# Operands of an expert layer's matmuls laid at an offset that changes from block to block, with two result buffers instead of three

## The chip, the cores and the metric

The kernel runs on one core of a Trainium2 chip, as one launch. The metric is device microseconds of the whole program, the median of three runs. TensorE multiplies, ScalarE (ACT) and VectorE (DVE) do elementwise work, GpSimd (POOL) issues the gathers and scatters by row index, SyncE (SP) issues the other transfers.

## The reference

Three layers in a row over 8 batches of 576 tokens, 512 wide: a linear attention, a mixture of experts of which each token takes two, and a soft mixture. The change lies in the second:

```python
for e in range(E):                       # 8 experts, w1[e] 512 x 1024, w2[e] 1024 x 512
    for k in range(2):
        mask = top2[:, k] == e
        h = np.maximum(x[mask] @ w1[e], 0.0)
        out[mask] += top2_w[mask, k, None] * (h @ w2[e])
```

Everything is float32. The kernel reaches that precision with three cheaper products: each factor is split into a rounded high part and the low rest, and high x high, low x high and high x low are added.

## The kernel before, in words

The routing makes lists of token rows, by expert. A block is the work of one expert on two tiles of 128 rows (three tiles in the blocks called three-tile blocks, which take in odd tiles). There are ten such blocks mixed in with the attention of later batches, then up to eight three-tile blocks under nested conditions, then fourteen blocks and up to sixteen more under conditions. How many run depends on the data.

One block, `block(b, n_s, n, n_n)` at line 872, goes through eight weight slices `u`. Slices 0 to 3 are the first layer: `hidden` (line 822) multiplies a quarter of w1 with the transposed rows `xh`, `xl`, 24 matmuls of 256 columns a slice, with the weights as the stationary operand and the rows as the moving one. ScalarE writes the high part `hh` (line 833) and VectorE the low part `hl` (line 834); with both, the PSUM bank is free again. In a three-tile block `hidden1` (line 836) does the third tile's rows, 12 matmuls a slice. There are three PSUM banks for these products, taken in turn, so that in a three-tile block the third tile's matmuls of slice 1 write the bank that `hh` and `hl` of slice 0 have read. Slices 4 to 7 are the second layer: `result` (line 854) multiplies `hh`, `hl` (stationary) with a quarter of w2 (moving), 12 matmuls of 512 columns a slice for two tiles.

Each weight slice comes by DMA into a ring, and `split` (line 793) makes its two parts in one of three slots R0, R1, R2: ScalarE the high part `R0h`, VectorE the low part `R0l` (line 797). A slice takes the next slot, eight slices a block, so the order of the slots in a block repeats after three blocks. The next block's rows are gathered by index into `xg`, transposed on TensorE at slice 6 (line 815), and written to `xh`, `xl`.

At the end of a block, or inside the next one, `scatter` (line 862) scales a tile's result out of PSUM into a buffer `y` (VectorE, line 865), and GpSimd adds the buffer to the rows of the output in HBM (line 866). Pool `yp` has three buffers `y`; a new one waits until the scatter that reads its buffer has landed. Three-tile blocks do all their scatters at their own end.

The order of instructions on the engines comes from a scheduler that goes by the code's order, the tiles' dependencies and a model of times. Memory is taken in the order in which tiles are named (lines 767 to 777), each size rounded up to 32 bytes per partition: h and R2, then two small tiles of 32 bytes each, x, `xg0` with 2080 and one of 32 bytes, R0, R1, `xg1`.

Of the kernel before, what the change touches and what calls it, by code (L numbers as in the profile page):

```python
# [11 lines left out]
F32 = mybir.dt.float32  # L12
F16 = mybir.dt.float16
FR = mybir.dt.float32r
I32 = mybir.dt.int32
# [6 lines left out]
P = 128  # L22
B, H, S, DH = 8, 8, 576, 64
D = H * DH
# [6 lines left out]
XC = D + E  # L31


NPA, NPB, NST, NTR = 10, 30, 14, 8
# [710 lines left out]
def experts(k, att, rs):  # L745

    nc, tc = k.nc, k.tc
    with ExitStack() as ctx:
        wp = ctx.enter_context(tc.tile_pool(name="wp", bufs=1, side="right", reuse_waits="tile"))
        yp = ctx.enter_context(tc.tile_pool(name="yp", bufs=2, side="right", reuse_waits="tile"))  # L750
# [4 lines left out]
        def bank(n, shape):  # L755
            b = banks[n]
            b.append(b.pop(0))
            return b[-1][0].tile(shape, F32, name=b[-1][1])
# [5 lines left out]
        w1 = k.w1.rearrange("e (c p) (u f) -> e u p c f", p=P, f=256)  # L764
        w2 = k.w2.rearrange("e (u c p) d -> e u p c d", c=2, p=P)
        tile = lambda n, s, d=FR: wp.tile([P] + s, d, name=n)
        hh, hl = [tile(f"h{h}", [8, 256]) for h in "hl"]
        R = [[None, None] for _ in range(NR)]
        R[2] = [tile(f"R2{h}", [1024]) for h in "hl"]
        gn, gc = [tile(n, [3], F32) for n in ("gn", "gc")]  # L770
        xh, xl = [tile(f"x{h}", [4, 256]) for h in "hl"]

        xg = [tile("xg0", [XC], F32)]
        nb = wp.tile([1, 2], I32, name="nb")
        R[0] = [tile(f"R0{h}", [1024]) for h in "hl"]
        R[1] = [tile(f"R1{h}", [1024]) for h in "hl"]
        xg.append(tile("xg1", [XC], F32))
        x3, h3 = [], []
        nc.vector.memset(gn, 0.0)
        regs = [nc.sync.alloc_register(f"er{i}") for i in range(2)]  # L780
# [17 lines left out]

        ys, late, puts = [], [], {}

        THREE = NPA + NPB + 1

        def at(b, s):
            t, c = (k.idxa, 2 * b + s) if b < NPA else (k.idx, 2 * (b - NPA) + s) if b < THREE else (k.idx3, 3 * (b - THREE) + s)
            return t[:, c:c + 1]
# [3 lines left out]

        def xpose(b, s):  # L810
            pt = bank("ph", [P, 4, P])
            h, l = [x[:, :, s * P:(s + 1) * P] for x in (xh, xl)] if s < 2 else x3
            rows = xg[s] if b else k.xg0[s]
            for c in range(4):
                nc.tensor.transpose(pt[:, c, :], rows[:, c * P:(c + 1) * P], k.ident)  # L815
            nc.scalar.activation(h, pt, AF.Copy)
            last = nc.vector.tensor_sub(l, pt, h.bitcast(F32))
            sc = yp.tile([P, E], F32, name="sc")
            with tc.issue_after(last.ins):
                nc.vector.scalar_tensor_tensor(sc, rows[:, D:XC], 1.0, k.eoha[:, b, :] if b < NPA else k.eoh[:, b - NPA, :], op0=ALU.mult, op1=ALU.mult, accum_out=gn[:, s:s + 1])  # L820

        def hidden(b, u):

            w = [x.rearrange("p (c f) -> p c f", c=4) for x in slot[b, u]]
            ph = bank("ph", [P, 2, 256])
            for g in range(2):
                n = 0
                for c in range(4):
                    for (i, x) in ((0, xh), (0, xl), (1, xh)):
                        nc.tensor.matmul(ph[:, g, :], w[i][:, c, g * P:(g + 1) * P], x[:, c, :], start=n == 0, stop=n == 11)  # L830
                        n += 1
            fs = slice(2 * u, 2 * u + 2)
            nc.scalar.activation(hh[:, fs, :], ph, AF.Relu)  # L833
            nc.vector.scalar_tensor_tensor(hl[:, fs, :], ph, 0.0, hh[:, fs, :].bitcast(F32), op0=ALU.max, op1=ALU.subtract)  # L834
# [18 lines left out]

        def result(b, u, py):
            w = [x.rearrange("p (c f) -> p c f", c=2) for x in slot[b, u]]
            order = [(f, s) for f in range(2) for s in range(len(py))]
            for f, s in order if u < 7 else sorted(order, key=lambda x: x[1]):
                a = [x[:, 2 * (u - 4) + f, s * P:(s + 1) * P] for x in (hh, hl)] if s < 2 else [x[:, 2 * (u - 4) + f, :] for x in h3]
                for (n, (h, i)) in enumerate(((0, 0), (0, 1), (1, 0))):
                    nc.tensor.matmul(py[s], a[h], w[i][:, f, :], start=u == 4 and f == n == 0, stop=u == 7 and f == 1 and n == 2)  # L860

        def scatter(b, s, py):
            y = yp.tile([P, D], F32, name="y", bufs=3)
            ys.append(y)
            nc.vector.tensor_scalar(y, py, gc[:, s:s + 1], None, op0=ALU.mult)  # L865
            d = nc.gpsimd.indirect_dma_start(out=k.x2[:NTOK // 2] if b < NPA else k.x2, out_offset=bass.IndirectOffsetOnAxis(ap=at(b, s), axis=0), in_=y, in_offset=None, compute_op=ALU.add)  # L866

            for o in puts.get(b, []):
                tc.declare_no_dep(d.ins, o.ins, reason="other rows")
            puts.setdefault(b, []).append(d)  # L870

        def block(b, n_s, n, n_n):

            expert(n)
            for s in range(n_n):
                gather(n, s)

            ahead = [(b, 2), (b, 3), (b, 4), (b, 5), (b, 6), (b, 7), (n, 0), (n, 1)]
            if n_s == 3:
                ahead = [(b, 2, 2), (b, 3, 0), (b, 4, 1), (b, 7, 2), (b, 5, 0), (b, 6, 1), (n, 0, 0), (n, 1, 1)]  # L880
            for u in range(8):
                split(*ahead[u])
                if u == 0:
                    load(n, 0)
                    load(n, 1)
                if u < 6:
                    load(n, ahead[u][1])
                if u < 4:
                    hidden(b, u)
                    if n_s == 3:  # L890
                        hidden1(b, u)
                else:
                    if u == 4:
                        py = [bank(f"py{s}", [P, D]) for s in range(n_s)]
                    if u == XU:
                        for s in range(n_n):
                            xpose(n, s)
                    result(b, u, py)
                if u == 1:
                    finish()  # L900
                    nc.vector.tensor_copy(gc, gn)
                yield
            late.extend((b, s, py[s]) for s in range(n_s))
            if b == NPA - 1 or b >= NPA + NST - 1:
                finish()

        def finish():
            while late:
                scatter(*late.pop(0))

        def whole(*a):
            for _ in block(*a):
                pass
# [6 lines left out]
        for s in range(2):  # L920
            xpose(0, s)
        n_steps, n_parts, n_done = len(MIX.split()), 0, 0
        for b in range(NPA):
            if b == NPA - 1:
                nc.gpsimd.tensor_copy(nb, ys[-1][0:1, 0:2].bitcast(I32))
                nc.gpsimd.tensor_copy(nb, k.nb)
            for _ in block(b, 2, *((b + 1, 2) if b + 1 < NPA else (THREE, 3))):
                n_parts += 1
# [20 lines left out]
        with ExitStack() as more:  # L949
            for i in range(NTR):  # L950
                more.enter_context(tc.If(n_threes > i))
                whole(THREE + i, 3, THREE + i + 1, 3)
        threes.close()
# [385 lines left out]
@with_exitstack  # L1339
def attention_moe_softmoe(ctx: ExitStack, tc: tile.TileContext, q, k, v, w_gate, w_noise, noise, w1, w2, phi, m1, m2, out):  # L1340
    s = K()
    s.tc, s.nc = tc, tc.nc
    s.q, s.k, s.v, s.w_gate, s.w_noise, s.noise, s.w1, s.w2 = q, k, v, w_gate, w_noise, noise, w1, w2
    s.phi, s.m1, s.m2, s.out = phi, m1, m2, out
    dp = ctx.enter_context(tc.tile_pool(name="dram", bufs=1, space=DRAM))
    s.xtab = dp.tile([NTOK + NFREE * P, XC], F32, name="xtab")
    s.x2 = dp.tile([NTOK + NFREE * P, D], F32, name="x2")
    s.ctx, s.n_regs = ctx, 0
    consts(s, ctx)
    att = attention(s)  # L1350
    next(att)
    rs = ctx.enter_context(tc.tile_pool(name="rs", bufs=1, side="right", reuse_waits="tile"))
    experts(s, att, rs)
    tail(s, rs, s.rg)
# [49 lines left out]
```

## Time and profile before

| | |
|---|---|
| median of three runs | 1219.99 us (1219.71 to 1221.48) |
| the profiled execution | 1222.69 us, its span 1221.0 us |
| TensorE, weight loads | 1125.1 and 984.7 us busy (92%, 81%) |
| VectorE, ScalarE, GpSimd | 799.3, 570.8, 324.6 us busy (65%, 47%, 27%) |
| mean granted clock of TensorE | 0.967 of full speed |
| blocks of two tiles alone | from about 647 to 1090 us |

A row of a group of instructions names engine, line, operation, what is written from what, and the shape. Matmuls are pipelined: one lasts longer than the distance to the next one's start, and it is the distance that counts for the time. The profile's "busy" of TensorE is thus not a measure of its rate. In the chain of waits each piece is work, or a wait for a transfer, that the end of the program depended on.

### The profile page before, as it was taken

The numbers are of one execution on the slowest core, as the hardware profiler recorded it, in microseconds if no ns is written. First come the engines' busy times: TensorE is split into PE (matmuls) and PEld (weight loads), VectorE is DVE, ScalarE is ACT, GpSimd is POOL, SyncE is SP. The second block draws the span as 40 slices with busy tenths as digits, with TensorE's granted clock in tenths as the row PEclk, the third lists the DMA queues.
The fourth block names the chain that finished last, engine by engine and source line by source line (L and its number), as shares of the span: only waits on it lengthen the run. The fifth ranks groups of instructions, "written<-read, shape, count | busy, mean of one in ns | idle before, by whom it ended". The sixth has DMA issues, their size and how long they took to land. (4 is left out here: it accounts for less than half of the span.)

```text
span 1221.0 us, 21167 instructions
## 1 busy us (share of the span) xinstructions
PE 1125.1 (92%) x7804; PEld 984.7 (81%) x7804; DVE 799.3 (65%) x1383; ACT 570.8 (47%) x877; POOL 324.6 (27%) x348
## 2 busy tenths in 40 slices
PE   2898859999999999999989999999999999969994
PEld 1787759998889999888968998998998998956542
DVE  7899778666976665554546666666666666645653
ACT  3575355465544544334434454544454454424324
POOL 4442153222244222211223322322321321210000
PEclk8899779999999999999999999999999999988997
DMA  9998162875536566555667564563745253237797
GB/s 327 297 318 306 45 207 77 242 227 157 141 84 189 135 199 172 139 149 163 174 184 249 138 202 106 150 195 84 223 110 173 47 148 84 43 66 295 265 356 310
DMA packets 116104, 219.08 MB, mean 179 GB/s; under 512 B 13968, under 2 KB 54032, under 8 KB 111888
## 3 DMA queue, kind: packets, MB, share of 16 engines
q1 hardware_dynamic: 98944, 177.11, 42.3%
q0 software_dynamic: 17040, 40.44, 16.8%
q8 instruction: 67, 1.10, 0.4%
q14 instruction: 53, 0.43, 0.1%
HBM read 243.31 MB, written 49.70 MB: 240 GB/s over the span
## 5 line engine op out<-in xcount | busy, mean ns | idle before, releaser
L797 DVE TENSOR_TENSOR R1l<-ringS,R1h 128x1024 fp32r<-128x1024 f32 x96 | 117.8, 1227 | 105.8 <-ACT R1h L797 103.3
L797 DVE TENSOR_TENSOR R0l<-ringS,R0h 128x1024 fp32r<-128x1024 f32 x95 | 116.8, 1229 | 100.8 <-ACT R0h L797 100.5
L797 ACT ACTIVATE R1h<-ringS 128x1024 fp32r<-128x1024 f32 x96 | 101.9, 1061 | 144.3 <-PE py L860 85.1
L797 DVE TENSOR_TENSOR R2l<-ringS,R2h 128x1024 fp32r<-128x1024 f32 x91 | 112.0, 1231 | 84.1 <-ACT R2h L797 81.7
L797 ACT ACTIVATE R0h<-ringS 128x1024 fp32r<-128x1024 f32 x95 | 100.8, 1061 | 137.9 <-PE py L860 77.0
L797 ACT ACTIVATE R2h<-ringS 128x1024 fp32r<-128x1024 f32 x91 | 96.5, 1061 | 136.2 <-PE py L860 75.1
L830 PE MATMUL ph<-xl,R0h 128*128 128x256 f32 x400 | 111.7, 279 | 1.5 <-issue 1.5
L830 PE MATMUL ph<-xh,R0h 128*128 128x256 f32 x400 | 112.0, 280 | 1.0 <-DVEq L949 1.0
L830 PE MATMUL ph<-xh,R0l 128*128 128x256 f32 x400 | 111.5, 279 | 0.0
L834 DVE SCALAR_TENSOR_TENSOR hl<-ph,hh 128x512 fp32r<-128x512 f32 x140 | 95.7, 684 | 23.2 <-ACT hh L833 23.2
L830 PE MATMUL ph<-xh,R1h 128*128 128x256 f32 x360 | 101.1, 281 | 8.1 <-DVE sc L820 7.6
L742 POOL DMA_INDIRECT xg<-xtab,pl_idx x40 | 50.3, 1257 | 215.9 <-DVE sc L820 197.6
L830 PE MATMUL ph<-xh,R2h 128*128 128x256 f32 x360 | 100.9, 280 | 0.5 <-DVE hl L834 0.5
L830 PE MATMUL ph<-xl,R1h 128*128 128x256 f32 x360 | 100.7, 280 | 0.0
L830 PE MATMUL ph<-xh,R1l 128*128 128x256 f32 x360 | 100.5, 279 | 0.0
L830 PE MATMUL ph<-xl,R2h 128*128 128x256 f32 x360 | 100.5, 279 | 0.0
L830 PE MATMUL ph<-xh,R2l 128*128 128x256 f32 x360 | 100.3, 279 | 0.0
L866 POOL DMA_INDIRECT x<-y,pl_idx x40 | 64.1, 1602 | 127.9 <-DVE y L865 117.8
L833 ACT ACTIVATE hh<-ph 128x512 fp32r<-128x512 f32 x140 | 81.6, 583 | 31.7 <-PE ph L830 31.7
L860 PE MATMUL py<-R1l,hh 128*128 128x512 f32 x200 | 79.7, 398 | 0.0
L860 PE MATMUL py<-R1h,hl 128*128 128x512 f32 x200 | 79.0, 396 | 0.0
L830 PEld LDWEIGHTS ph<-xh,R0h 128*128 128x128 f32 x400 | 75.7, 189 | 2.3 <-issue 1.6
(441 smaller groups left out, 3011.0 us busy)
## 6 DMA issues: line engine op xcount, KB each, us to landing
ringS<-in_moe_w_dram SPq DMA_DIRECT2D x292, 512.0 KB
ringA<-in_moe_w_dram SPq DMA_DIRECT2D x12, 1024.0 KB
ringA<-in_moe_w_dram SPq DMA_DIRECT2D x22, 512.0 KB
xtab<-xr SPq DMA_DIRECT2D x36, 256.0 KB
kt<-in_k_dram SPq DMA_DIRECT2D x8, 1024.0 KB
v<-in_v_dram SPq DMA_DIRECT2D x8, 1024.0 KB
x<-z SPq DMA_DIRECT2D x5, 1280.0 KB
ringS<-x SPq DMA_DIRECT2D x5, 1024.0 KB
```

The costliest lines, as they stand in the source:

```text
L742: k.nc.gpsimd.indirect_dma_start(out=x, out_offset=None, in_=k.xtab[:n], in_offset=bass.IndirectOffsetOnAxis(ap=idx, axis=0))
L797: turn[1:] = [nc.scalar.activation(r[0], f, AF.Copy), nc.vector.tensor_sub(r[1], f, r[0].bitcast(F32))]
L830: nc.tensor.matmul(ph[:, g, :], w[i][:, c, g * P:(g + 1) * P], x[:, c, :], start=n == 0, stop=n == 11)
L833: nc.scalar.activation(hh[:, fs, :], ph, AF.Relu)
L834: nc.vector.scalar_tensor_tensor(hl[:, fs, :], ph, 0.0, hh[:, fs, :].bitcast(F32), op0=ALU.max, op1=ALU.subtract)
L860: nc.tensor.matmul(py[s], a[h], w[i][:, f, :], start=u == 4 and f == n == 0, stop=u == 7 and f == 1 and n == 2)
L866: d = nc.gpsimd.indirect_dma_start(out=k.x2[:NTOK // 2] if b < NPA else k.x2, out_offset=bass.IndirectOffsetOnAxis(ap=at(b, s), axis=0), i ...
```

## The change

The tiles `xh`, `xl` grow by 128 elements (512 bytes) and `hh`, `hl` too. Block `b` uses a view of them that starts 16 elements (64 bytes) times 0 to 7 into the tile: for the rows that number is `b % 8` (7 for the three-tile blocks and for the block behind them), for the first layer's outputs `(3 * b + b // 8) % 8` (0 for the three-tile blocks). The small tiles go to the end, so that h, R2, x, R0 and R1 all start at one remainder by 512 bytes. To make room, `y` has two buffers instead of three.

```diff
-        hh, hl = [tile(f"h{h}", [8, 256]) for h in "hl"]
+        ht = [tile(f"h{h}", [2048 + 128]) for h in "hl"]
         R = [[None, None] for _ in range(NR)]
         R[2] = [tile(f"R2{h}", [1024]) for h in "hl"]
-        gn, gc = [tile(n, [3], F32) for n in ("gn", "gc")]
-        xh, xl = [tile(f"x{h}", [4, 256]) for h in "hl"]
-
-        xg = [tile("xg0", [XC], F32)]
-        nb = wp.tile([1, 2], I32, name="nb")
+        xt = [tile(f"x{h}", [1024 + 128]) for h in "hl"]
         R[0] = [tile(f"R0{h}", [1024]) for h in "hl"]
         R[1] = [tile(f"R1{h}", [1024]) for h in "hl"]
-        xg.append(tile("xg1", [XC], F32))
+        xg = [tile(f"xg{s}", [XC], F32) for s in range(2)]
+        gn, gc = [tile(n, [3], F32) for n in ("gn", "gc")]
+        nb = wp.tile([1, 2], I32, name="nb")
+
+        def x_of(b):
+            o = 16 * (7 if b == NPA or b >= THREE else b % 8)
+            return [x[:, o:o + 1024].rearrange("p (c t) -> p c t", c=4) for x in xt]
+
+        def h_of(b):
+            o = 16 * (0 if b >= THREE else (3 * b + b // 8) % 8)
+            return [h[:, o:o + 2048].rearrange("p (f t) -> p f t", f=8) for h in ht]
+
+        THREE = NPA + NPB + 1
...
-            h, l = [x[:, :, s * P:(s + 1) * P] for x in (xh, xl)] if s < 2 else x3
+            h, l = [x[:, :, s * P:(s + 1) * P] for x in x_of(b)] if s < 2 else x3
...
+            (xh, xl), (hh, hl) = x_of(b), h_of(b)
...
+            hh, hl = h_of(b)
...
-            y = yp.tile([P, D], F32, name="y", bufs=3)
+            y = yp.tile([P, D], F32, name="y", bufs=2)
```

No engine's instructions change their order. What does change is what a `y` waits for. On VectorE, at the end of a three-tile block, before (`DMASW` and a number is one of the counters that scatters and gathers raise when they land; 4700 to 4702 are the results of the three tiles):

```order
L797 TENSOR_TENSOR R1l<-ringS,R1h 128x1024 [waits DMAHW0_49,Activation_49]
L865 TENSOR_SCALAR y<-py_4700,gc 128x512 [waits DMASW0_49,PE_49]
L865 TENSOR_SCALAR y<-py_4701,gc 128x512 [waits DMASW1_49,PE_49]
L865 TENSOR_SCALAR y<-py_4702,gc 128x512 [waits DMASW2_49,PE_49]
L949 COMPARE_AND_BRANCH
L901 COPY gc<-gn 128x3 [waits DVE_49]
L797 TENSOR_TENSOR R2l<-ringS,R2h 128x1024 [waits DMAHW1_49,Activation_49]
L834 SCALAR_TENSOR_TENSOR hl<-ph,hh 128x512 [waits Activation_49]
```

and of the change:

```order
L805 TENSOR_TENSOR R1l<-ringS,R1h 128x1024 [waits DMAHW0_49,Activation_49]
L873 TENSOR_SCALAR y<-py_4700,gc 128x512 [waits DMASW1_49,PE_49]
L873 TENSOR_SCALAR y<-py_4701,gc 128x512 [waits DMASW2_49,PE_49]
L873 TENSOR_SCALAR y<-py_4702,gc 128x512 [waits DMASW6_49,DVE_49,PE_49]
L957 COMPARE_AND_BRANCH
L909 COPY gc<-gn 128x3 [waits DVE_49]
L805 TENSOR_TENSOR R2l<-ringS,R2h 128x1024 [waits DMAHW1_49,Activation_49]
L841 SCALAR_TENSOR_TENSOR hl<-ph,hh 128x512 [waits Activation_49]
```

The order is the same. The third `y` waits for a counter of a later transfer: the scatter of the first `y` of the same block, where it was one of the block before.

## Rows read from the trace of the kernel before

**Rows 1.** Windows: stretch, then busy us of each engine, clock, DMA share, GB/s

```profile
647.00:1090.00 443.00, 440.32 (x2892) 398.53 (x2890) 286.76 (x402) 216.44 (x266) 120.14 (x105) 1.00 0.50 135
```

**Rows 2.** Chain of waits, 660 to 760 us: start, us, what

```profile
671.12 10.89 PE ph L830 x96
682.00 3.21 PE py L860 x14
...
685.54 2.33 PE py L860 x10
...
688.42 5.56 PE py L860 x24
693.97 11.21 PE ph L830 x96
...
717.18 11.31 PE ph L830 x96
```

**Rows 3.** TensorE in order of time, 700 to 705 us: start, duration, what

```profile
699.95 0.28 PE L830 MATMUL ph<-xl,R2h 128*128 128x256 f32 x1
...
702.18 0.28 PE L830 MATMUL ph<-xh,R2l 128*128 128x256 f32 x1
702.30 0.28 PE L830 MATMUL ph<-xh,R0h 128*128 128x256 f32 x1
...
704.91 0.28 PE L830 MATMUL ph<-xh,R0l 128*128 128x256 f32 x1
```

**Rows 4.** TensorE in order of time, 758 to 763 us

```profile
758.09 0.39 PE L860 MATMUL py<-R1h,hl 128*128 128x512 f32 x1
...
760.19 0.40 PE L860 MATMUL py<-R1h,hl 128*128 128x512 f32 x1
...
761.58 0.39 PE L860 MATMUL py<-R2h,hl 128*128 128x512 f32 x1
...
762.72 0.39 PE L860 MATMUL py<-R2l,hh 128*128 128x512 f32 x1
```

**Rows 5.** Groups by line and shape: count, then busy us, mean ns, idle before

```profile
L830 PE MATMUL ph<-xh,R0h 128*128 128x256 f32 x400 | 112.0, 280 | 1.0 <-DVEq L949 1.0
...
L830 PE MATMUL ph<-xh,R1h 128*128 128x256 f32 x360 | 101.1, 281 | 8.1 <-DVE sc L820 7.6 <-DVE bf L490 0.3 <-DVE hl L834 0.2
L830 PE MATMUL ph<-xh,R2h 128*128 128x256 f32 x360 | 100.9, 280 | 0.5 <-DVE hl L834 0.5
```

**Rows 6.** VectorE in order of time, 543 to 554 us, a three-tile block's end

```profile
545.42 0.75 DVE L865 TENSOR_SCALAR y<-py,gc 128x512 f32<-128x512 f32 x1 [0.49 <-PE py L860]
...
546.51 1.23 DVE L797 TENSOR_TENSOR R2l<-ringS,R2h 128x1024 fp32r<-128x1024 f32 x1
548.88 0.69 DVE L834 SCALAR_TENSOR_TENSOR hl<-ph,hh 128x512 fp32r<-128x512 f32 x1 [1.15 <-ACT hh L833]
```

**Rows 7.** GpSimd in order of time, 543 to 554 us

```profile
544.55 1.62 POOL L866 DMA_INDIRECT x<-y,pl_id  x1 [26.22 <-DVE y L865]
```

**Rows 8.** TensorE in order of time, 551 to 553 us

```profile
552.21 0.28 PE L843 MATMUL ph<-R1h,x3h 128*128 128x256 f32 x1
```

**Rows 9.** Line 866, the first scatter at 508.9 us, then at 580.2 us

```profile
DMA to landing us min/median/max: 6.0/6.0/6.0
...
DMA to landing us min/median/max: 4.8/4.8/4.8
```

**Rows 10.** Chain of waits, 440 to 640 us; last, VectorE in order of time

```profile
615.93 0.44 POOL x L866
...
619.74 10.69 DMA x<-y,pl_id
...
637.25 0.52 PE ph L815 x3
...
616.78 0.75 DVE L865 TENSOR_SCALAR y<-py,gc 128x512 f32<-128x512 f32 x1 [0.48 <-PE py L860]
```

**Rows 11.** DMA issues: tiles, queue, count, median us to landing

```profile
x<-y,pl_idx POOLq DMA_INDIRECT x40, 4.9
```

More of the change, by code (lines that the diff above doesn't have):

```diff
@@ L799, in experts @@
         ys, late, puts = [], [], {}
-        THREE = NPA + NPB + 1
         def at(b, s):
```

## The prediction, made before the change was run

> **What bounds the kernel now.** I read first the busy times by stretch, then the chain of waits, then single engines in order of time. In the stretch from 647 to 1090 us, twenty blocks of two row tiles each, TensorE is busy 440.32 of 443 us at full granted clock [rows 1]; the chain of waits there holds nothing but its lines 815, 830 and 860 [rows 2]. So in this stretch, and nearly so in the ten interleaved blocks before it, time is the number of matmuls times the distance from one start to the next. That distance is the first thing to look at: the work of the first layer (96 matmuls, always the same shapes, at the same clock) takes 10.89 us in one block, 11.21 in the next and 11.31 in the one after [rows 2]. Inside one block the starts are (702.18 - 699.95) / 19 = 117 ns apart on slot R2 and (704.91 - 702.30) / 23 = 113 ns apart on R0 right behind it [rows 3]. In the second layer they are (760.19 - 758.09) / 9 = 233 ns apart on R1, and (762.72 - 761.58) / 5 = 228 ns on R2 [rows 4]. No engine is waited for in any of these rows. What differs from block to block is the order in which the three weight slots come up (period three), so where the operands lie does touch the rate, by some 4% at most between the rows seen.
>
> **Part 1: addresses.** The change issues the same instructions in the same order on every engine; it moves operands. Before, by the sizes of the tiles in their order, h and R2 share a remainder by 512 bytes, x lies 64 bytes past it, R0 and R1 128 past it. The first layer (weights stationary, x moving) therefore sees distances of +64 and -64 bytes, the second (h stationary, weights moving) 0 and +128. After, all share one remainder and the distance is 64 times 0 to 7, another one in each block. Three matmuls for each of 400 + 360 + 360 uses of a slot [rows 5] make 3360 in the first layer, by 96 that is 35 blocks run, and 35 x 48 = 1680 in the second for the first two row tiles. Of the 35 blocks, 13 have one of the two old distances in the first layer and 22 have one that no row shows.
>
> The bounds from rows: if every block came out like the best seen, the first layer would take 10.89 instead of the mean of the three kinds, (10.89 + 11.21 + 11.31) / 3 = 11.14 us: 0.25 x 35 = 8.8 us less. If every block came out like the worst, 0.17 x 35 = 6.0 us more. For the second layer the mean is (3.21 + 2.33 + 5.56) / 48 = 231 ns [rows 2]: at 228 everywhere 3 x 1680 = 5.0 us less, at 233 everywhere 3.4 us more. Together -13.8 to +9.4 us. Which end is nearer? Slots R0, R1 and R2 all occur in the fast kind of first-layer block and all in the slow kind, so the distance alone does not choose the rate; the run-up to a block does too. Then eight distances should give a mixture much like the old one. I take 0 and keep both ends.
>
> On this the Trainium skill ("SBUF — State Buffer", section "Who interferes with whom") has a rule: TensorE reads moving operand and weights through two independent ports and waits on no one. By the rule the term is 0 for any layout; the 10.89 and 11.31 above, for equal work, show that it can't be the whole story. The skill's back-to-back formula ("TensorE: Matmul & The Clock Gate", section "Back-to-back issue gap") gives about 109 ns for 256 columns and 216 for 512, under every row here; by it, an estimate from that page, a layout with no loss at all would save some 50 us, which no distance seen so far comes near.
>
> **Part 2: the y buffers go from three to two.** Each row tile's result goes from PSUM through `y` to a scatter, and a new `y` has to wait until the scatter that read its buffer has landed. In blocks of two tiles the buffer comes round after a whole block, some 23 us, while a scatter lands in 4.9 us (median) [rows 11]: no cost. In a block of three tiles the third `y` takes the buffer of the first one of the same block. There VectorE writes the third `y` at 545.42, as soon as TensorE is done [rows 6]; the first scatter is issued only at 544.55 [rows 7] and lands 4.8 to 6.0 us later in the two cases that the trace resolves [rows 9]. The third `y` therefore starts at 549.4 to 550.6, 4.0 to 5.1 us late, and with it all that stands behind it on VectorE: the copy of the gates, the low half of weight slot R2, and the subtraction `hl` that also gives a PSUM bank back. `hl` at present starts at 548.88, with slack. Queued up without gaps it ends 3.0 us after the start of `y` (R2l ends at 546.51 + 1.23 = 547.74, that is 2.32 after 545.42; 0.69 for `hl`): 552.4 to 553.6. The bank is wanted by the third tile's matmuls of the second weight slice, at 552.21 [rows 8]. So TensorE stalls 0.2 to 1.4 us in each of four such ends of block (there are five blocks of three, the fifth is below); VectorE has caught up one weight slice later. Four times: 0.8 to 5.6, and between two landings as near I take the middle, 3.2 us.
>
> At the end of the fifth the same wait is on the chain itself. GpSimd issues the three scatters from 615.93, the third at 619.74 behind the `y` of 616.78; the chain then waits 10.69 us for this one to land, for GpSimd leaves the conditional blocks only when all its transfers are in, gathers the next rows, and TensorE's next transposes stand until 637.25 [rows 10]. With two buffers the third `y` starts at 615.93 + 4.8 to 6.0, ends 0.75 later, and its scatter goes out 0.27 later still: 621.8 to 623.0 instead of 619.74, 2.0 to 3.2 us late. If the 10.69 us are mostly a full queue, less of that comes through. I take 2.0, bounds 0 and 3.2.
>
> The rest costs nothing on the path. A few waits at the start of the last stage and on one early gather change their order or their count, but the loads there wait for the same last scatters. VectorE and ScalarE write the same bytes at other places.
>
> **The sum.** 0 + 3.2 + 2.0 = 5.2 us, bounds -13.8 + 0.8 + 0 to 9.4 + 5.6 + 3.2, that is -13 to +18. Against the profiled execution, 1222.69 us (a span of 1221.0 and 1.7 around it), 1227.9; that execution lies 2.7 above the median of the three runs, 1219.99, so I forecast 1219.99 + 5.2 = 1225.2 for the median.
>
> **The rivals.**
> First, the offsets do not average out but help: with all slots on one remainder a block keeps its fast state through all four slices instead of falling from 113 to 117 ns at a change of slot. For it speaks the third kind of block, which changes state within itself [rows 3]; against it, blocks whose slots alternate run at one rate throughout. If every block comes out like the best ones, -13.8 + 5.2 = -8.6, 1211.4. It decides from half-way on: the mean distance in the first layer, counted alone, has to fall by (5.2 + 2.4) / 3.36 = 2.3 ns before the whole is faster by more than 0.2%.
> Second, the change is not felt: scatters land at the early end (4.8 us), TensorE stalls 0.2 us and the last scatter waits in a full queue either way. Then 4 x 0.2 + 0 and no effect of addresses: 1220.8. For it speaks that the stall is 0.2 at one of only two landings resolved; against it, that the other gives 1.4.
> Third, distances not seen before are bad ones: first layer always at 11.31, second at 233 ns, and the waits in full: 9.4 + 8.8 = 18.2, 1238.2. Against it, the four distances seen lie within 4% of each other; for it, that the other four are unknown.
>
> **How the numbers follow.** What a measurement of this kernel can tell is about 0.2%, 2.4 us. I give the forecast (1222.5 to 1230, the waits between their bounds and a few us from the offsets) 0.45, the helpful offsets 0.20, no effect 0.20, bad offsets 0.15. A part of the helpful case is eaten by the waits and ends within 2.4 us, a part of the unfelt one falls outside; so faster 0.18, same 0.22, slower 0.60. The range for 8 in 10 reaches past the forecast's own into both offset cases: 1211 to 1235.
>
> **What would show it.** In the profile after: third `y` of each three-tile block begun 4 to 5 us after TensorE is done, its releaser a scatter; a gap of up to 1.4 us in front of the third tile's matmuls of the second slice; the transposes at the exit 0 to 3 us later. For the offsets: the 96 first-layer matmuls per block between 10.9 and 11.3 us whatever the block's number. A block at 10.5 or at 12 would prove me wrong about the offsets, and no wait before the third `y` would prove me wrong about the buffers.

## The result, and the profile after

| | before | after |
|---|---|---|
| median of six runs each, side by side | 1219.89 us (1217.65 to 1221.48) | 1226.15 us (1224.22 to 1228.14) |
| the profiled execution | 1222.69 us | 1226.0 us, its span 1224.3 |
| mean granted clock of TensorE | 0.967 | 0.971 |

The ratio is 1.0052, with a 95% interval of 1.0038 to 1.0067: slower by 6.3 us, 4.6 to 8.2. The forecast was 1225.2.

The stretch of two-tile blocks comes first. Windows, kernel after, same columns as in [rows 1]:

```profile
647.00:1090.00 443.00, 443.00 (x2891) 401.39 (x2889) 285.26 (x401) 216.45 (x266) 118.42 (x103) 1.00 0.50 135
```

TensorE is without a gap and at full clock, as before, so a loss here is one of rate. The chain of waits of the kernel after, 670 to 775 us, four blocks and the start of a fifth (start, us, what):

```profile
670.44 11.52 PE ph L837 x96
...
688.44 5.60 PE py L868 x24
694.04 11.31 PE ph L837 x96
...
711.74 5.45 PE py L868 x24
717.19 11.52 PE ph L837 x96
...
735.11 5.51 PE py L868 x24
740.62 10.91 PE ph L837 x96
...
757.97 5.59 PE py L868 x24
763.57 11.51 PE ph L837 x96
```

These are blocks 12 to 16, with the rows at 4, 5, 6, 7 and 0 times 64 bytes, and the outputs at 5, 0, 3 and 6 in the first four. Before, a first layer took 10.89 to 11.31 us [rows 2]; now there is a third kind of 11.5. The last 24 second-layer matmuls take 5.45 to 5.60. From the starts of all matmuls I took the mean distance from one to the next (distances over 150 and 270 ns, in which something else lies between, left out), by the block's offset in units of 64 bytes:

| offset | 0 | 1 | 2 | 3 | 4 | 5 | 6 | 7 |
|---|---|---|---|---|---|---|---|---|
| first layer, ns, by that of the rows | 119.9 | 117.8 | 119.2 | 115.1 | 119.9 | 117.8 | 119.1 | 115.1 |
| second layer, ns, by that of the outputs | 228.6 | 233.3 | 232.9 | 229.7 | 229.0 | 233.3 | 232.8 | 229.8 |

(Two-tile blocks and mixed ones; the three-tile blocks have 115.9 and 229.9.) The change was a survey without meaning to be: offsets 0 to 3 and 4 to 7 repeat each other, so the distance counts by its remainder by 256 bytes. Over all 3360 first-layer matmuls the mean goes from 115.95 to 117.61 ns, 5.6 us more; over the 1800 of the second layer from 231.45 to 230.93, 0.9 less. Addresses so cost 5.58 - 0.94 = 4.6 us.

Then the third `y`. VectorE in order of time, kernel after, at the end of the third three-tile block and of the fifth (in brackets the idle time before and what ended it):

```profile
543.78 1.40 DVE L873 TENSOR_SCALAR y<-py,gc 128x512 f32<-128x512 f32 x2
549.69 0.75 DVE L873 TENSOR_SCALAR y<-py,gc 128x512 f32<-128x512 f32 x1 [4.51 <-DMA x<-y,pl_id]
550.48 0.17 DVE L909 COPY gc<-gn 128x3 f32<-128x3 f32 x1
550.55 1.23 DVE L805 TENSOR_TENSOR R2l<-ringS,R2h 128x1024 fp32r<-128x1024 f32 x1
551.70 0.68 DVE L841 SCALAR_TENSOR_TENSOR hl<-ph,hh 128x512 fp32r<-128x512 f32 x1
...
614.78 1.40 DVE L873 TENSOR_SCALAR y<-py,gc 128x512 f32<-128x512 f32 x2
620.94 0.75 DVE L873 TENSOR_SCALAR y<-py,gc 128x512 f32<-128x512 f32 x1 [4.76 <-DMA x<-y,pl_id]
```

Where [rows 6] had the third `y` 0.49 us behind TensorE, it now waits for a scatter. (In the first of the five blocks the profile names a matmul as what ended the wait, but the scatter of the first `y` lands there at 477.26, and the third `y` starts at 477.39.) `hl` ends at 551.70 + 0.68 = 552.38. TensorE in order of time, kernel after, where the bank that `hl` gives back is wanted, in the second and the third of these blocks, and at the exit:

```profile
516.92 0.39 PE L850 MATMUL ph<-R1h,x3h 128*128 128x256 f32 x1 [1.04 <-DVE hl L841]
...
552.50 0.32 PE L850 MATMUL ph<-R1h,x3h 128*128 128x256 f32 x1
...
621.89 0.55 PE L837 MATMUL ph<-xh,R0h 128*128 128x256 f32 x1 [5.30 <-DVEq L957]
622.25 0.41 PE L837 MATMUL ph<-xl,R0h 128*128 128x256 f32 x1
```

In the third block TensorE goes on without a wait (compare [rows 8]); in the second, whose first scatter took 6.0 us to land, it stalls for 1.04 us. At the exit it waits 5.30 us for VectorE's branch at line 957, which stands behind the third `y`, and the 24 matmuls that follow start 213 ns apart. Windows of the kernel after, columns as above, show why: behind the pause the granted clock stands at the lower of its two levels, 1.2 GHz, for these 24, which costs 24 x 100 ns = 2.4 us.

```profile
621.90:627.10 5.20, 5.20 (x24) 5.20 (x25) 1.40 (x2) 1.06 (x1) 1.56 (x1) 0.50 0.74 205
627.20:635.00 7.80, 7.80 (x70) 7.80 (x70) 4.77 (x5) 4.64 (x6) 1.78 (x2) 0.99 0.72 214
```

In the kernel before, TensorE stood at the exit in two short pauses and later, for the gathered rows, in a long one, and there too a stretch at the lower clock followed, behind the long one (TensorE in order of time, then a window):

```profile
617.74 0.36 PE L830 MATMUL ph<-xh,R0h 128*128 128x256 f32 x1 [0.99 <-DVEq L949]
619.60 0.28 PE L830 MATMUL ph<-xl,R0h 128*128 128x256 f32 x1 [1.50 <-issue]
...
637.25 0.52 PE L815 MATMUL ph<-ident,xg 128*128 128x128 f32 x3 [3.48 <-DMA xg<-xtab,pl_idx]
...
638.50:641.90 3.40, 3.40 (x11) 2.62 (x10) 0.00 (x0) 0.50 (x1) 0.00 (x0) 0.50 0.18 65
```

GpSimd in order of time, kernel after:

```profile
621.97 1.56 POOL L874 DMA_INDIRECT x<-y,pl_id  x1 [2.66 <-DVEq L957]
632.92 1.02 POOL L742 DMA_INDIRECT xg<-xtab,pl_idx  x1 [9.39 <-PE ph L837]
```

The third scatter goes out 2.2 us later than in [rows 10]. The transposes that stood until 637.25 there start at 638.63 now, without a wait: TensorE has lost its time earlier. From its last matmul before the exit to the first one of block 11 it takes 30.72 us, before 30.90.

### The profile page after: what moved, and what is told of

It reads as the page before. It is cut to its first block, busy times and chain, and to the rows that moved or that the text cites. A ratio compares the mean times of both kernels' runs of the same rounds, so it can differ in the third digit from the quotient of the medians.

```text
span 1224.3 us, 21167 instructions
## 1 busy us (share of the span) xinstructions
PE 1127.1 (92%) x7804; PEld 986.5 (81%) x7804; DVE 798.6 (65%) x1383; ACT 571.3 (47%) x877; POOL 328.7 (27%) x348
## 5 line engine op out<-in xcount | busy, mean ns | idle before, releaser
L805 DVE TENSOR_TENSOR R1l<-ringS,R1h 128x1024 fp32r<-128x1024 f32 x96 | 117.8, 1227 | 106.7 <-ACT R1h L805 103.5
```

The lines of the kernel that those rows point to most:

```text
L805: turn[1:] = [nc.scalar.activation(r[0], f, AF.Copy), nc.vector.tensor_sub(r[1], f, r[0].bitcast(F32))]
```

## The experiments

Theory A: the 6.3 us are mostly addresses; the distance of moving and stationary operand by 256 bytes sets the rate, together with how the layer before ended (the run-up). Theory B, the forecast's: addresses average out, the waits for `y` are the price. The kernels ran in three sets, each with the kernel before on the same chip, which took 1219.96, 1220.05 and 1220.39 us there; differences are against the median of the own set.

**Two buffers alone** (kernel before, `y` with `bufs=2`).

```diff
-            y = yp.tile([P, D], F32, name="y", bufs=3)
+            y = yp.tile([P, D], F32, name="y", bufs=2)
```

> The kernel before with two buffers y instead of three, every address as before by remainder. Theory A (most of the 6.3 us are addresses, the waits cost little): third y of the three-tile blocks 4 to 6 us late, one TensorE stall of about 1 us, exit unchanged; 0.9 us slower than before, at most 2.5. Theory B (the forecast's: the waits are the price): 5.2 us slower, 3 to 9.

Measured 1224.79 us, ratio 1.0046 (1.0026 to 1.0065): 4.8 slower (3.2 to 7.9), on the side of B. VectorE in order of time:

```profile
506.27 1.41 DVE L865 TENSOR_SCALAR y<-py,gc 128x512 f32<-128x512 f32 x2
513.71 0.75 DVE L865 TENSOR_SCALAR y<-py,gc 128x512 f32<-128x512 f32 x1 [6.03 <-DMA x<-y,pl_id]
```

and TensorE, the one stall of over 0.4 us in the three-tile blocks, and the exit:

```profile
516.45 0.38 PE L843 MATMUL ph<-R1h,x3h 128*128 128x256 f32 x1 [1.34 <-DVE hl L834]
...
622.42 0.55 PE L830 MATMUL ph<-xh,R0h 128*128 128x256 f32 x1 [5.17 <-DVEq L949]
```

So A in its first form is wrong about the waits: they do cost.

**The same two buffers, the wait taken away.** The third tile's result goes through the third gather buffer, which is free at that point (the diff is against the kernel with two buffers alone):

```diff
-            y = yp.tile([P, D], F32, name="y", bufs=2)
+            y = yp.tile([P, D], F32, name="y", bufs=2) if s < 2 else xg[2][:, :D]
```

> The kernel with two buffers y and the addresses of before, but the third tile's result goes through the third gather buffer, which is free then, so that the third y waits for no scatter. If the 4.8 us of two buffers were the third y's wait: no stall in the three-tile blocks, exit as before, within 1.5 us of before. Rival (the 4.8 us lie elsewhere, in later stages or memory): still 3 to 6 us slower.

Measured 1220.43 us, ratio 1.000 (0.9985 to 1.0015), no slower than before within 1.8 us. VectorE in order of time:

```profile
503.65 1.41 DVE L865 TENSOR_SCALAR y<-py,gc 128x512 f32<-128x512 f32 x2
505.54 0.75 DVE L865 TENSOR_SCALAR xg<-py,gc 128x512 f32<-128x512 f32 x1 [0.48 <-PE py L860]
```

The wait is gone and all of the 4.8 us with it: it was the third `y`.

**Fixed layouts, three buffers.** Only the order of the tiles in memory differs from the kernel before (the two small tiles take 64 bytes together); the instructions and their order are the same. In short, each line lists the tiles in their new order:

```diff
 # rows 64 bytes below the slots, outputs at the slots' remainder:
+        xh, xl;  gn, gc;  R0, R1, R2;  hh, hl;  xg0, xg1;  nb
 # rows and outputs 64 bytes below:
+        xh, xl;  hh, hl;  gn, gc;  R0, R1, R2;  xg0, xg1;  nb
 # rows at the slots' remainder, outputs 64 bytes above:
+        xh, xl;  R0, R1, R2;  gn, gc;  hh, hl;  xg0, xg1;  nb
```

> Fixed layout, three buffers y: rows start 64 bytes below the remainder (by 512) of all weight slots, first-layer outputs on the slots' own remainder. Theory A with a run-up (distance by 256 bytes sets the rate, and a block whose last second-layer slice ran at distance 0 starts the next first layer at 118 ns): second layer 228.5 ns in the mean, 5.0 us less; first layer 117.3 to 117.8, 4.6 to 6.2 us more; net -1 to +2 us. Theory A without a run-up (distance alone): first layer 113.3, second 226.7, 9 and 8 us less, together -17. Theory B (addresses average out, only waits cost): first layer 116.0 as before, net 0.

Measured 1218.87 us, ratio 0.9993 (0.9975 to 1.001). Chain of waits:

```profile
716.09 11.31 PE ph L830 x96
727.39 3.18 PE py L860 x14
...
733.75 5.48 PE py L860 x24
```

> As the last, but rows and first-layer outputs both 64 bytes below the slots' remainder. Theory A with a run-up: first layer 113.3 to 113.8 ns (7.2 to 8.9 us less), second 229.5 (3.3 us less), together 11 us faster than before, about 1209. Theory A without a run-up: the same, 11 us faster, with the first layer at 113.3 throughout. Theory B: no difference, within 2.4 us.

Measured 1211.77 us, ratio 0.9936 (0.9913 to 0.9959), 8.2 us faster than before (5.0 to 10.6), somewhat less than the 11 of Theory A. Chain of waits:

```profile
710.08 10.91 PE ph L830 x96
720.99 3.20 PE py L860 x14
...
727.38 5.51 PE py L860 x24
```

> The layout that the trace of the change shows as worst: rows on the slots' own remainder, first-layer outputs 64 bytes above it. Theory A: first layer 120 ns (4 x 3360 = 13.4 us more), second 233.3 (3.1 us more), together 16.5 us slower, about 1236. Theory B: no difference, within 2.4 us.

Measured 1235.57 us, ratio 1.0123 (1.0097 to 1.015), 15.6 us slower. Chain of waits:

```profile
697.86 11.51 PE ph L830 x96
709.37 3.27 PE py L860 x14
...
715.84 5.61 PE py L860 x24
```

Equal work at equal clock in an equal order: 10.91 against 11.51 us by addresses alone. Theory B's "no difference" falls three times, the first time in the rows only: there the first layer at 11.31 eats what the second gains, as A with a run-up had said. In all three layouts the rows are the first tiles in memory, and it is the weights that lie 64 bytes lower in the last; in the change the weights stay and the rows move. So the first layer's rate follows the distance between the two, not the place of either.

The Trainium skill ("SBUF — State Buffer", section "Who interferes with whom") gives TensorE two independent read ports, one for the moving operand and one for the weights, and says that it never waits on anyone. The page speaks of engines that get in each other's way and has nothing on addresses; the 10.91 and 11.51 do not fit two operands that are independent at any layout, and the measurement decides.

**One part of the change alone,** with its two buffers: only the rows' offset changes, then only that of the outputs.

```diff
-            o = 16 * (0 if b >= THREE else (3 * b + b // 8) % 8)
+            o = 0
```

> The change with the offset of the first-layer outputs fixed at 0 and that of the rows left changing; two buffers y. Theory A (distance by 256 bytes sets the rate, and a second layer ending at distance 0 starts the next first layer at 118 ns): first layer 118.3 ns in the mean, 7.9 us more; second layer 228.6, 4.8 us less; the two buffers 2.5 to 4.8 us: 5.6 to 7.9 slower than before. Theory B (addresses average out): first layer 116.0, time as with two buffers alone, 4.8 slower.

Measured 1226.52 us, ratio 1.0048 (1.003 to 1.0067): 6.5 slower. That interval, 3.7 to 8.2 us, leaves Theory B's 4.8 standing; the first layer's mean distance, 118.15 ns where B has 116.0, does not.

```diff
-            o = 16 * (7 if b == NPA or b >= THREE else b % 8)
+            o = 16 * 7
```

> The change with the offset of the rows fixed at 7 (64 bytes below the slots' remainder, by 512) and that of the outputs left changing; two buffers y. Theory A: first layer 113.3 ns except behind blocks whose outputs are at distance 0 or 256 (7 of 30) and in the three-tile blocks, 114.9 in the mean, 3.5 us less; second layer 230.9, 0.9 us less; two buffers 2.5 to 4.8: between 1.9 faster and 0.4 slower than before. Theory B: 4.8 slower.

Measured 1218.93 us, ratio 0.9992 (0.9975 to 1.0009): 1.1 faster (3.1 faster to 1.1 slower), which excludes B's 4.8 slower. It is the rows' changing offset that does the harm. Chain of waits of the second one, blocks 13 to 16, with the outputs at 0, 3 and 6 in the first three:

```profile
690.06 10.90 PE ph L837 x96
...
707.34 5.49 PE py L868 x24
712.83 11.31 PE ph L837 x96
...
730.54 5.50 PE py L868 x24
736.03 11.30 PE ph L837 x96
...
753.78 5.58 PE py L868 x24
759.36 10.89 PE ph L837 x96
```

With the rows always at 7, the first layer still has two rates, and the layer before chooses: behind outputs at 0 or 4 all four such blocks of the last nineteen run at 11.31, behind 1, 2, 5 or 6 all nine at 10.9, behind 3 or 7 three and three. My "113 except behind 0 or 256" was right for the first two and wrong for the third.

**Can both layers be fast?** Rows 64 bytes below; of the outputs only those of the last slice 64 below, the rest at 0 (two tiles for `h` in place of one); then the same with the third tile's rows and outputs moved by two paddings of 192 bytes.

```diff
+        xh, xl;  hb (last slice);  gn, gc;  R0, R1, R2;  ha (first three);  xg0, xg1;  nb
```

> Fixed layout, three buffers: rows 64 bytes below the slots, the outputs that slices 4 to 6 read on the slots' own remainder, those that slice 7 reads 64 bytes below. Theory A (only the last slice before the next first layer decides how that starts): first layer 113.3 ns in the blocks of two tiles, 114.5 in the mean, 4.9 us less; second layer 228.9, 4.6 us less; 9.5 us faster than before, about 1210.4. Rival: most of the second layer decides: first layer 117.8 as with all outputs at distance 0, net 1 us faster.

Measured 1219.34 us, ratio 0.9987 (0.9976 to 0.9998). A fell here: the chain of waits has

```profile
712.96 11.31 PE ph L830 x96
...
730.62 5.50 PE py L860 x24
```

> As the last, and the third tile's rows and outputs 64 bytes above and 256 below the slots' remainder, so that the moving operand lies 64 bytes below the stationary one in its first layer and at distance 256 in its second. Theory A: 240 matmuls at up to 4.5 ns less, and the first-layer slices behind them at 113.3 too: 1 to 3 us faster than the last kernel. Rival: the three-tile blocks are bound by VectorE or are unaffected: no difference to it.

Measured 1218.6 us, ratio 0.998 (0.9965 to 0.9995). The three-tile blocks come 35.4 us apart instead of 35.6, too little to be told from the last kernel in time.

**Two last versions:** both at 64 below, with the paddings; and the outputs of slices 4 and 5 at 0, of 6 and 7 at 64 below, with the paddings.

```diff
+                wt.tile([P, 48], F32, name="pad0")   # before x3
+                wt.tile([P, 48], F32, name="pad1")   # before h3
```

> Rows and first-layer outputs both 64 bytes below the slots (as in the layout that was 8.2 us faster), three buffers, and the third tile's rows and outputs 64 bytes above and 256 below the slots. Theory A: as that layout and 0.2 us less in each three-tile block: 9 to 10 us faster than before, about 1210.5. Rival (the gain of that layout came from its chip and day, addresses average out): within 2.4 us of before.

Measured 1211.8 us, ratio 0.9929 (0.9909 to 0.9949): the gain of that layout holds on another chip.

> As the last, but the outputs that slices 4 and 5 read lie on the slots' own remainder. Second layer 229.0 ns in the mean, 2 us less than in the last kernel. Whether the next first layer starts at 113 or 118 ns: if the step of the three-matmul cycle at which the second layer ends decides, either; at 113.3 about 11 us faster than before, at 117.8 about 2 us faster. The trace tells which.

Measured 1211.27 us, ratio 0.9925 (0.9906 to 0.9944): the fastest, 9.1 us faster than before and some 15 under the change, though not to be told from the kernel ahead of it. Chain of waits:

```profile
708.75 10.91 PE ph L830 x96
...
726.03 5.51 PE py L860 x24
```

**The ledger.** For every kernel: mean distances as above, what they make against the kernel before over 3360 and 1800 matmuls, the measured difference of medians, and what is left. The distances are those of one profiled execution of each kernel.

| kernel | buffers y | first, ns | second, ns | addresses, us | measured, us | left, us |
|---|---|---|---|---|---|---|
| the change | 2 | 117.61 | 230.93 | +4.6 | +6.3 | 1.6 |
| two buffers alone | 2 | 115.93 | 231.45 | -0.1 | +4.8 | 4.9 |
| rows only | 2 | 118.15 | 228.87 | +2.8 | +6.5 | 3.7 |
| outputs only | 2 | 115.17 | 230.82 | -3.7 | -1.1 | 2.6 |
| wait taken away | 2 | 115.92 | 231.44 | -0.1 | 0.0 | 0.1 |
| rows 64 below, outputs 0 | 3 | 116.90 | 228.99 | -1.2 | -1.1 | 0.1 |
| both 64 below | 3 | 114.49 | 230.21 | -7.1 | -8.2 | -1.1 |
| rows 0, outputs 64 above | 3 | 119.81 | 233.23 | +16.2 | +15.6 | -0.6 |
| last slice 64 below | 3 | 116.79 | 229.38 | -0.9 | -0.7 | 0.2 |
| and third tile | 3 | 116.85 | 228.85 | -1.7 | -1.4 | 0.3 |
| both 64, third tile | 3 | 114.51 | 230.01 | -7.5 | -8.6 | -1.1 |
| half 64 below | 3 | 114.43 | 229.35 | -8.9 | -9.1 | -0.2 |

Where the third `y` does not wait, the distances alone give the time to about 1 us, from -9 to +16. Where it waits, 1.6 to 4.9 us are left, 3.2 in the mean. That is the change: 4.6 us of addresses and 1.6 (in the mean of such kernels 3.2) of waits.

The stages of the traces bear this out. The table has the time from the first matmul of the first three-tile block to the end of the last one before the exit, from there to block 11, and from the first matmul of block 11 to the end of the last of block 29:

| kernel | three-tile blocks, us | exit, us | blocks 11 to 29, us |
|---|---|---|---|
| before | 178.59 | 30.9 | 439.67 |
| wait taken away | 178.59 | 29.0 | 439.67 |
| two buffers alone | 181.06 | 29.9 | 439.68 |
| the change | 179.10 | 30.7 | 442.99 |

In blocks 11 to 29 TensorE has no gap in any of the four: two buffers cost nothing there, the addresses 3.3 us. In the three-tile blocks the waits cost 2.5 us at the old addresses. In the change they cost 1.6, and the addresses give 1.1 back (a block without a stall takes 35.47 us instead of 35.69). So the 4.6 us of addresses and the 4.8 of two buffers alone do not add up in the change: 9.4 lies outside its 4.6 to 8.2. It is the 4.8 (3.2 to 7.9) that looks high, for the stages show only 2.5 of it and, against the kernel with the wait taken away, 0.9 more at the exit.

## Why the prediction came out right, and which steps did not

**The sum** was 5.2 and came out at 6.3, but two terms were off and by luck made up for each other.

**Part 1, addresses, taken as 0: mis-sized.** It measured +4.6 us. The step that failed is "eight distances should give a mixture much like the old one". The old layout held only odd distances (+64 and -64 bytes in the first layer), which are the two fast kinds; of the thirty blocks of two tiles the change puts fourteen at an even offset, where no row of before had looked, and these run at up to 120.0 ns. The bounds were wrong for the same reason: they took the best and the worst block seen as ends for distances not seen. The 4.6 lies inside them only because the bad distances are mixed with others; a fixed layout of bad ones costs 16.2 us, where the upper bound was 9.4. In the second layer, where the old layout held distances of 0 and 128, the bounds held. "96 first-layer matmuls between 10.9 and 11.3 us whatever the block's number" is refuted by 11.52. Right was that distance alone does not choose: the run-up does too, where the rows lie 64 bytes below the weights.

**Part 2, blocks of three tiles, taken as 3.2: the mechanism right, the size too large.** The third `y` waits for a scatter in all five, 4.4 to 5.8 us. But of the four ends only one stalls TensorE visibly, by 1.04 us, and all four together lengthen the stage by 1.6 us (2.5 with two buffers alone). My early landing (4.8 us) gave 0.2 us of stall; in the row at 552.50 `hl` is done at 552.38, just in time. The four kernels with the wait have one stall each, of 0.92 to 1.34 us.

**Part 2, the exit, taken as 2.0: moved rather than added.** The third scatter is 2.2 us later, within 2.0 to 3.2. What I missed is the branch: VectorE's decision at line 957 is queued behind the third `y`, so TensorE stands 5.30 us at once, where it had two pauses of 0.99 and 1.50 before, and the lower clock follows it. In return it no longer waits for the gathered rows, and the lower clock that followed that wait before does not come. Before, that later wait was 3.48 us in the execution profiled; in the other kernels with three buffers it was 0.43 to 3.45. From TensorE's last matmul before the exit to block 11 the four kernels with the wait take 29.4 to 30.7 us and the nine without 27.9 to 31.8 (means 30.1 and 29.4), so a cost of the exit is not to be told from what varies anyway. Taking the wait away gave back 4.8 us by the medians; the traces account for 2.5 of it in the three-tile blocks and at most some 0.9 at the exit, and where the rest lies stays open.

**The rivals.** The first, that one remainder for all slots keeps a block at its fast rate, is wrong: with all slots on one remainder the blocks from 11 on do keep one rate, but which one depends on the distance and the run-up. With rows and outputs both 64 bytes below, the last eighteen blocks all have 10.91 us; with the rows there and the outputs at 0 they have 11.31, and with the rows at 0 and the outputs 64 above 11.51. The third, bad offsets, was the right mechanism for half of the blocks, and 1235.57 is what a layout made only of them takes. The second, not felt, is excluded by the interval.

**Open:** why a first layer behind outputs at 64 bytes below starts fast in some blocks and slow in others. "Last slice 64 below" (11.31) and "half 64 below" (10.91) have the same last slice, so that slice alone does not decide; at the ends of those second layers the distances run in a cycle of three (226, 229, 231 ns), and the two kernels leave it at different steps. In the traces step and rate go together without exception. Of the last nineteen blocks of two tiles in each kernel, 103 have rows 64 bytes below the weights (by the remainder by 256) behind outputs that lie so too: in 60 the last matmul of the second layer stands 230 to 236 ns ahead of the next, and these run at 113.4 to 113.6 ns; in 43 it stands 226 or 227 ahead, and these run at 117.8. No kernel set the step by itself, so whether it is the cause or only goes along with the cause was not tested.

## What to carry over

Rates that differ between rows of equal work bound only the cases in those rows: count which values of the moved quantity the trace has seen before calling the rest an average of them. In a kernel bound by back-to-back float32 matmuls, lay the moving operand at one fixed, measured distance from the stationary one rather than at many. When a buffer is taken away, list everything queued behind the first instruction that will wait, branches too.

## What the runs showed of the hardware

At full granted clock a matmul of 256 columns follows the last one after 113.3 or 117.8 ns with the moving operand at an odd multiple of 64 bytes from the stationary one (always 117.8 in the change at +64, either at -64; in the kernel before, slot R2 at +64 ran at 113.3 as well, in blocks whose other slots lie at -64), and after some 118.5 to 120.0 at an even one. One of 512 columns follows after 226.7 ns at distance 0 in the steady slices (229.0 in the mean of the layout that is all at 0), 228.8 at 64 bytes with the stationary operand below, and about 233.3 at 64 above or at 128, all by the remainder by 256; transposes in between raise a few. Neither slot nor place in the program matters beside that: the blocks of one kind repeat these numbers from 640 to 1090 us.
